# Values' products bound behind a feed-forward row, and the last weight splits put one in a slot

## The chip, the cores and the metric

The kernel runs on one core of one Trainium2 chip. The metric is the device time of one execution in microseconds. The kernel before takes 693.66 us, the median of three runs (693.4 to 695.26).

A core has five engines that run side by side, each through its own list of instructions in order: PE (TensorE, matrix products; its weight loads are shown apart as PEld), DVE (VectorE), ACT (ScalarE), POOL (GpSimd) and SP (SyncE, which issues the DMAs here). An engine that waits holds up all that stands behind in its list.

## The reference

Attention with four sink keys and a window of 128 keys, for 4 batches of 8 heads, 768 positions and 64 dimensions, and then a feed-forward layer on its output as 3072 tokens of 512 values:

```python
keep = is_sink | in_window                    # pos < 4, or 0 <= rel < 128
scores = np.where(keep, scale * q @ k.T, -1e9)
a = softmax(scores)
x = (a @ v).transpose(0, 2, 1, 3).reshape(3072, 512)
h = x @ w_in                                  # 512 x 2048
sp = np.maximum(h, 0.0) + np.log1p(np.exp(-np.abs(h)))
g = h * erf(sp)
return g @ w_out                              # 2048 x 512
```

## The kernel before

**Tiles and stages.** The tokens are worked in 12 groups of 256 (`g`; three groups make a batch). A group's attention takes four *steps*, one for each pair of heads, so that there are 48 steps `s`. Its feed-forward part takes 16 *rows* (`f`), one for each 128 of the 2048 hidden values; rows are counted through as `m = 16 * g + f`.

A step goes through all engines. PE makes the scores (`ps`, L420). DVE puts masks on them and takes the row's extreme (L433, L438), ACT the exponentials and their sum (L442, four a step), DVE divides by the sum (L454 to L476). From step 12 on DVE turns the result in blocks (`turn`, L489 and L490), and two DMAs through DRAM (`pd<-turn`, L492; `pa<-pd`, L518) finish the turn. POOL masks the two triangles of the window into `pz` and `pa` (L529, L533, L542). Then PE makes the values' products (`av`, L584), and ACT and DVE split them into a high and a low part (`xh`, L603; `xl`, L604), which are the input of the feed-forward rows of that group.

A row is 12 hidden products (`h`, L797: four parts of 128, three products of high and low each). Two rows share one buffer `h`, of which there are two, so a pair of rows needs the buffer of the pair but one before: ACT (L814) and DVE (L817) must have read that. ACT (L814 to L820) and DVE (L817, L821) make the activation of two rows; DVE casts its high part (L828) and POOL subtracts for the low part (L829, `g`). Four rows later come the projections (`o`, L844 to L846, six for a row), which sum up in two banks for each group; ACT copies them out (L850) before the next group uses the banks.

**The weights** are 32 blocks: 0 to 15 of `w_in`, 16 to 31 of `w_out`. Products of the first rows use them whole (`wf`); later ones use a high and a low part (`wt`), which `wsplit` makes once for each block: a cast on ACT (L708) and a subtract on DVE (L709). The table `split` says in which row that is due.

**The order.** Rows are written in slots `a = m + 10`. Each part of a slot is written under a priority (`at`), and a scheduler then sets every engine's order by priority and by when it thinks that the inputs are ready. `follow(prev, ins)` adds to that: `ins` comes after `prev`, with no wait on the chip where both are on one engine. `core(s)` writes the values' products of step `s - 2` and behind them the scores of step `s`; from step 8 on, step `s` has its slot at `a = 4 * s - 12`. In `av` the products are chained with `follow`; `prev` is what the first of them must come behind. `mark` keeps named instructions for that.

Of the kernel before, what the change touches and what calls it, by code (L numbers as in the profile page):

```python
# [39 lines left out]
NE, AL = 4, 2  # L40
# [3 lines left out]
DT = 10  # L44

TT, T2 = 12, 15

NSINK = 22

LATE = 31  # L50

FH = 8
# [10 lines left out]
def kernel(  # L63
# [11 lines left out]
    nc = tc.nc  # L75
# [3 lines left out]
    NPAIR = H // 2  # L79
    NC = DM // P  # L80
    NF = DF // P
# [59 lines left out]
    def fast_path():  # L141
        with ExitStack() as st:
# [64 lines left out]
            xp, early = {}, {}  # L207

            stp = {}
            mark = {}  # L210
            first, turn = [], []
# [127 lines left out]
            def warm(o, n):  # L339

                for _ in range(n):
                    nc.tensor.transpose(out=o, in_=ident, identity=ident)

            def follow(prev, ins):

                if prev is not None:
                    tc.add_manual_dep(
                        ins.ins, prev.ins.name,
                        mybir.DependencyInfo(mybir.DependencyClass.NoSync, mybir.DependencyReason.DATA), reason="order",
                    )  # L350
                return ins
# [23 lines left out]
            def core(s):  # L375

                prev = mark.get(("p", s - 1)) if s - AL == 3 * NPAIR - 1 else mark["av", s - 1] if s == 2 * NPAIR else None
                late = s - AL >= 2 * NPAIR and s - AL != 3 * NPAIR - 1
                if late:
                    prev = av(s - AL)  # L380
                if s < NSTEP:
                    score(s, prev)
# [63 lines left out]
            def turn_tile(tag):  # L446

                x = wpool.tile([P, 2 * DM], F32, name=f"turn_{len(turn)}", **tag)
                turn.append(x.rearrange("p (m t) -> p m t", t=P))
# [101 lines left out]
            def av(s):  # L551

                g, c = divmod(s, NPAIR)
                d = stp[s]
                gb = g % GPB
                if s < 2:
                    a = ps_h.tile([P, 2, GT], F32, tag="h", name=f"av_{s}")[:, 0, :]
                elif s < NE:
                    a = ps_o.tile([P, DM], F32, tag="o", name=f"av_{s}")[:, :GT]
                else:  # L560
                    a = ps_t.tile([P, GT], F32, tag="t", name=f"av_{s}")
                d["av"] = a
                vt, pz = d["v"], d["pz"]
                warm(a[:, :P], 6 if s < NE - 1 else 0)
                late = s >= TT and gb > 0
                pa = d["pa"].rearrange("p h i t -> p h (i t)")
                ops = []
                for j, (t0, t1) in enumerate(((0, HP), (HP, 3 * HP), (3 * HP, GT))):
                    if j > 0 or gb > 0:
                        x = vt[j] if isinstance(vt, list) else vt[:, j]  # L570
                        ops.append((x, pa[:, :, t0:t1], t0))
                if late:
                    ops = [ops[1], ops[0], ops[2]]
                for i in range(2):
                    for z, hf in enumerate((lo, hi)):
                        ops.append((vz[:, z, i, 2 * c : 2 * c + 2], pz[:, :, i, hf], P * i + HP * z))
                prev = mark.get(("p", s + 1)) if 0 < s < NE - 1 else None
                for m, (x, y, t0) in enumerate(ops):
                    for h in range(2):
                        o = a[64 * h : 64 * h + 64, t0 : t0 + y.shape[-1]]  # L580
                        with at(pos(s), "rest") if s >= TT and m + h > 0 else nullcontext():
                            prev = follow(
                                prev,
                                nc.tensor.matmul(  # L584
                                    o, x[:, h, :], y[:, h, :], start=(m == 0), stop=(m == len(ops) - 1), skip_group_check=True
                                ),
                            )
                mark["av", s] = prev
                return prev
# [16 lines left out]
            def at(a, what):  # L606

                key = int(a * PW) + O[what] + (E.get(what, 0) if a < EA else 0)
                return tc.high_priority(offset=tc.tile_snap_priority() + 1 - key)

            def pos(s):

                return s if s < NE else 3 * s - 6 if s < 2 * NPAIR else 4 * s - 12

            plan = {}
            for s in range(NSTEP + AL):
# [23 lines left out]
                if s < 2 * NPAIR:  # L640
                    x = pos(s) + (3 if s < NE else 5)
# [9 lines left out]
            def attn(a):  # L651

                for what, fn, s in sorted(plan.get(a, ()), key=lambda x: (STAGES.index(x[0]), x[2])):
                    with at(a, "prepl" if what == "prep" and s > TT else what):
                        fn(s)
# [3 lines left out]
            def need(n):  # L659
                return 4 * (n // 4) if n < 16 else n - 16 + LAG  # L660

            order = sorted(range(32), key=need)
            split = {}
            for n in range(32):
                x = n - 16
                split.setdefault(NF - 5 + n if x < 0 else NF + 6 + (x - FH) * 5 // 4 if x >= FH else 2 * NF - 1 + x * 2 // 3, []).append(n)

            def wload(n):

                src = wblock(n)  # L670
                t = staged[n] = wpool.tile([P, 2 * DM], I32, tag="wo", name=f"ws_{n}")
                if src.dtype == F32:
                    mark["wl"] = nc.sync.dma_start(t[:, :DM].bitcast(F32), src)
                else:
                    mark["wl"] = nc.sync.dma_start(t, src.bitcast(I32))
# [24 lines left out]
            def wsplit(n, m):  # L700

                t = wf[n]
                tag = dict(tag="wk", bufs=4) if n in (18, 20, 22) else dict(tag="wo")
                d = wt[n] = wpool.tile([P, 2, DM], F32R, name=f"wt_{n}", **tag)
                x, y = mlp.mark[min((m - 1) // 2, NF) - 1]
                if m >= LATE:
                    x, y = mark["e", 3 * NPAIR], mark["s", 3 * NPAIR]
                follow(x, nc.scalar.copy(d[:, 0, :], t))  # L708
                follow(y, nc.vector.tensor_tensor(d[:, 1, :], t, d[:, 0, :].bitcast(F32), op=ALU.subtract))  # L709

# [6 lines left out]
            mlp = make_mlp(work, ps_h, ps_o)  # L717
# [19 lines left out]
            for m in range(-LEAD, NG * NF + LAG + 2):  # L737
                a = m + LEAD
                live = 0 <= m < NG * NF
                if live:  # L740
                    g, f = divmod(m, NF)
                    if f % 2 == 0:
                        hp = mlp.hid_tile(m)
                    if f > 0:
                        with at(a, "hid"):
                            ahead = mlp.hidden(hp, xp[g], f)
                attn(a)
                if m == NF - 6:
                    turn_tile(dict(tag="wo"))
                w = m - LAG  # L750
                if 0 <= w < NG * NF:
                    g2, f2 = divmod(w, NF)
                    with at(a, "proj"):
                        mlp.project(gs[w // 2], g2, f2, lambda ins: follow(ahead if live and f and g >= 2 else None, ins))
                    if f2 == NF - 1:
                        for i in range(2):
                            r0 = (g2 * 2 + i) * P
                            with at(a, "res"):
                                nc.sync.dma_start(out[r0 : r0 + P, :], mlp.result(g2, i))
                if live:  # L760
                    if f == 0:
                        with at(a, "hid"):
                            mlp.hidden(hp, xp[g], f)
                    if f % 2 == 1:
                        with at(a, "act"):
                            gs[m // 2] = mlp.act(hp, m, m < NF + FH)

                while wn < 32 and a >= 1 and (wn < (0, 0, 3, 5)[a - 1] if a < 5 else wn < 2 * a - 4 or need(order[wn]) <= m + W1):
                    with at(a, "wc"):
                        wconv(order[wn], wn)  # L770
                    wn += 1
                    with at(a, "wl"):
                        for n in order[wl : wn + WQ]:
                            wload(n)
                            wl += 1
                for n in split.get(m, ()):
                    with at(a, "ws"):
                        wsplit(n, m)
# [74 lines left out]
    def general_path():  # L853

        NT_S = S // P
        with ExitStack() as st:
# [71 lines left out]
            with tc.tile_pool(name="g_one1", bufs=1) as one, tc.tile_pool(name="g_work1", bufs=2) as work:  # L928
# [3 lines left out]
                with tc.For_i(0, B, 1) as b:  # L932
                    for gb in range(GPB):
# [25 lines left out]
                        for i in range(2):  # L959
# [3 lines left out]
                            )  # L963

    fast_path()
    ok = nc.values_load(flagi[0:1, 0:1], min_val=0, max_val=1)
    with tc.If(ok == 0):
# [31 lines left out]
```

## Time and profile before

| | us |
|---|---|
| time, median of three runs | 693.66 |
| time of the profiled execution | 693.52 |
| its span on the core | 691.8 |
| PE busy in the span | 672.9 (97%) |
| ACT busy | 506.2 (73%) |
| DVE busy | 486.3 (70%) |
| POOL busy | 289.8 (42%) |

The span runs from the first to the last instruction of the profiled execution; 1.7 us of its time lie around it. Busy is time with an instruction of that engine at work. Matmuls overlap, and their ends are modelled, so two that follow each other are best measured from start to start. The granted clock of PE is 1.00 in nearly all of the span.

### The profile page before, as it was taken

The page shows a single profiled execution, that of the slowest core. Times are in us where ns is not written, and L with a number is a line of the kernel's source. Part 1 is how long each engine was busy: PE and PEld are TensorE (multiplying, and loading weights), DVE is VectorE, ACT ScalarE, POOL GpSimd, SP SyncE. Part 2 cuts the span into 40 slices and gives each one's busy share as a digit, 9 for nine tenths or more (in the row PEclk, how much of TensorE's full clock was granted, in tenths as well). Part 3 has the DMA queues.
Part 4 walks back from the last instruction along what each step waited for, and adds up shares of the span by engine and source line. Part 5 has one row for each costly group of instructions (what it writes and reads, how often), then busy time and mean ns, then how long its engine had stood idle before and what let it go on. Part 6 is the DMA issues. An engine that isn't in the chain of part 4 may idle for free.

```text
span 691.8 us, 16069 instructions
## 1 busy us (share of the span) xinstructions
PE 672.9 (97%) x5527; PEld 562.6 (81%) x5527; DVE 486.3 (70%) x1385; ACT 506.2 (73%) x1143; POOL 289.8 (42%) x510
## 2 busy tenths in 40 slices
PE   8899999999999999999999999999999999999996
PEld 5666567788787888898898898888898888899895
DVE  7999996769878788677685686577685678443241
ACT  5788668988876778687587587597596587587583
POOL 3422213133536545474464364355464364332231
PEclk9999999999999999999999999999999999999999
DMA  8999203114545655553553554353553464120001
GB/s 221 275 383 349 82 16 71 37 32 88 124 82 111 138 103 102 128 102 71 124 103 65 121 105 103 86 110 72 123 105 64 108 118 85 42 48 1 31 1 36
DMA packets 258873, 72.06 MB, mean 104 GB/s; under 512 B 224800, under 2 KB 250912, under 8 KB 258784
## 3 DMA queue, kind: packets, MB, share of 16 engines
q1 hardware_dynamic: 258224, 70.89, 44.0%
q8 instruction: 46, 0.75, 0.5%
q14 instruction: 43, 0.35, 0.2%
q10 hardware_dynamic: 560, 0.07, 0.1%
HBM read 51.25 MB, written 19.40 MB: 102 GB/s over the span
## 4 chain that ended last, share of the span: by engine, by line
PE 78%; DVE 8%; ACT 6%; DMA 4%; issue 2%; SPq 1%; POOL 1%; DVEq 0%; ACTq 0%; POOLq 0%
PE h L797 31%; PE o L844 10%; PE o L846 10%; PE o L845 10%; PE av L584 6%; PE ps L420 5%; PE o L841 3%; ACT pst L442 1%; DMA ws<-in_moe_w_out_dram 1%; DMA pa<-pd 1%; DMA pd<-turn 1%; PE h L793 1%; DVE wf L696 1%; DVE wf L693 1%; DVE pst L462 1%
## 5 line engine op out<-in xcount | busy, mean ns | idle before, releaser
L797 PE MATMUL h<-xh,wt 128*128 128x256 f32 x1408 | 271.8, 283 | 1.1 <-DVE w L817 1.1
L797 PEld LDWEIGHTS h<-xh,wt 128*128 128x128 f32 x1408 | 223.6, 188 | 17.8 <-issue 10.4
L797 PE MATMUL h<-xl,wt 128*128 128x256 f32 x704 | 196.5, 279 | 0.0
L829 POOL TENSOR_TENSOR g<-w,g 128x512 fp32r<-128x512 f32 x84 | 113.1, 1346 | 156.3 <-DVE g L828 155.2
L797 PEld LDWEIGHTS h<-xl,wt 128*128 128x128 f32 x704 | 132.5, 188 | 6.3 <-issue 2.4
L844 PE MATMUL o<-wt,g 128*128 128x512 f32 x336 | 131.9, 394 | 0.0
L845 PE MATMUL o<-wt,g 128*128 128x512 f32 x336 | 131.8, 392 | 0.0
L846 PE MATMUL o<-wt,g 128*128 128x512 f32 x336 | 129.0, 394 | 0.3 <-POOL g L829 0.3
L442 ACT ACTIVATE pst<-pst,neg 128x144 f32<-128x144 f32 x192 | 77.5, 405 | 55.9 <-DVE neg L438 55.6
L821 DVE SCALAR_TENSOR_TENSOR w<-u,w 128x512 f32<-128x512 f32 x84 | 73.9, 880 | 35.7 <-ACT u L820 35.6
L817 DVE SCALAR_TENSOR_TENSOR w<-w,h 128x512 f32<-128x512 f32 x84 | 56.7, 676 | 43.5 <-ACT w L816 41.0
L814 ACT ACTIVATE r<-h 128x512 f32<-128x512 f32 x96 | 57.0, 594 | 28.3 <-PE h L797 26.4
L828 DVE CAST g<-w 128x512 fp32r<-128x512 f32 x84 | 38.5, 458 | 52.8 <-PE o L846 49.6
L844 PEld LDWEIGHTS o<-wt,g 128*128 128x128 f32 x336 | 63.1, 188 | 12.5 <-issue 1.3
L846 PEld LDWEIGHTS o<-wt,g 128*128 128x128 f32 x336 | 62.3, 188 | 12.7 <-POOL g L829 0.7
L845 PEld LDWEIGHTS o<-wt,g 128*128 128x128 f32 x336 | 63.1, 188 | 9.6
L542 POOL TENSOR_SCALAR_AFFINE_SELECT pz<-pa 64x256 f32<-64x256 f32 (+1 forms) x96 | 43.8, 456 | 54.5 <-ACT pa L504 53.6
L820 ACT ACTIVATE u<-r 128x512 f32<-128x512 f32 x96 | 60.6, 632 | 6.1 <-DVE w L821 0.5
L816 ACT ACTIVATE w<-r 128x512 f32<-128x512 f32 x96 | 60.6, 631 | 3.2
L815 ACT ACTIVATE r<-r 128x512 f32<-128x512 f32 x96 | 60.6, 631 | 2.6
L819 ACT ACTIVATE r<-r 128x512 f32<-128x512 f32 x96 | 60.6, 632 | 2.4
L818 ACT ACTIVATE r<-r 128x512 f32<-128x512 f32 x96 | 60.5, 631 | 2.5
(107 smaller groups left out, 975.7 us busy)
## 6 DMA issues: line engine op xcount, KB each, us to landing
pd<-turn SPq DMA_DIRECT2D x36, 320.0 KB, 2.6
pa<-pd SPq DMA_DIRECT2D x144, 80.0 KB, 2.6
ws<-in_moe_w_in_dram SPq DMA_DIRECT2D x16, 512.0 KB, 6.6
ws<-in_moe_w_out_dram SPq DMA_DIRECT2D x16, 512.0 KB, 8.4
out_dram<-ot SPq DMA_DIRECT2D x24, 256.0 KB, 2.2
v<-in_v_dram SPq DMA_DIRECT2D x56, 96.0 KB, 2.6
kq<-in_k_dram SPq DMA_DIRECT2D x152, 32.0 KB, 1.9
kq<-in_q_dram SPq DMA_DIRECT2D x152, 32.0 KB, 2.2
```

The lines of the kernel that those rows point to most:

```text
L442: mark["e", s] = nc.scalar.activation(y, y, AF.Exp, bias=d["neg"][:, i, h : h + 1], scale=-1.0, accum_out=d["sum"][:, i, h : h + 1])
L797: last = nc.tensor.matmul(o, wt[NC * j + c][:, p, fs], xt[e][:, c, :], start=(m == 0), stop=(m == len(ops) - 1))
L815: nc.scalar.activation(r, r, AF.Square, bias=b_v, scale=-0.5)
L816: nc.scalar.activation(w, r, AF.Square, bias=b_w)
L818: nc.scalar.activation(r, r, AF.Square, bias=b_r)
L819: nc.scalar.activation(r, r, AF.Square, bias=b_q)
L820: sq = nc.scalar.activation(u, r, AF.Square, bias=b_u, scale=CK**0.5)
L821: pr = nc.vector.scalar_tensor_tensor(out=acc, in0=u, scalar=CU0 * CK, in1=acc, op0=ALU.add, op1=ALU.mult)
L829: nc.gpsimd.tensor_tensor(gl, acc, gh.bitcast(F32), op=ALU.subtract)
L844: behind(nc.tensor.matmul(o, gh[:, ws], wt[16 + f][:, 0, :], start=(f == 0), stop=False))
L845: nc.tensor.matmul(o, gh[:, ws], wt[16 + f][:, 1, :], start=False, stop=False)
L846: nc.tensor.matmul(o, gl[:, ws], wt[16 + f][:, 0, :], start=False, stop=(f == NF - 1))
```

## The change

It does four things. The values' products of steps 12 to 19 are put behind the last product of the hidden row that was written last before them (`mark["h"]`), in the same slot; they had no such bound. The blocks 16 to 23 become due in rows 30 to 37, one a row, where it was rows 31 to 35. Each split's cast and subtract follow the activation of the pair of rows before its own; a cap on that, and a rule that put all splits due from row 31 on behind the softmax of step 12, are gone. And the tile that step 12 turns into (`turn_0`) is allocated under the priority of the splits, with a memset of eight of its columns on POOL.

```diff
+BL = 20
@@ av
-                prev = mark.get(("p", s + 1)) if 0 < s < NE - 1 else None
+                prev = mark.get(("p", s + 1)) if 0 < s < NE - 1 else mark["h"] if TT <= s < BL else None
@@ the table split (NF = 16, FH = 8)
-                split.setdefault(NF - 5 + n if x < 0 else NF + 6 + (x - FH) * 5 // 4 if x >= FH else 2 * NF - 1 + x * 2 // 3, []).append(n)
+                split.setdefault(NF - 5 + n if x < 0 else NF + 6 + (x - FH) * 5 // 4 if x >= FH else 2 * NF - 2 + x, []).append(n)
@@ wsplit
-                x, y = mlp.mark[min((m - 1) // 2, NF) - 1]
-                if m >= LATE:
-                    x, y = mark["e", 3 * NPAIR], mark["s", 3 * NPAIR]
+                x, y = mlp.mark[(m - 1) // 2 - 1]
@@ the slots
-                            ahead = mlp.hidden(hp, xp[g], f)
+                            ahead = mark["h"] = mlp.hidden(hp, xp[g], f)
                 attn(a)
                 if m == NF - 6:
-                    turn_tile(dict(tag="wo"))
+                    with at(a, "ws"):
+                        turn_tile(dict(tag="wo"))
+                        nc.gpsimd.memset(turn[0][:, 5, :8], 0.0)
```

The scheduler orders the engines anew with this. The names in the rows below are the tiles': `av_12` belongs to step 12, `h_36` to rows 36 and 37, `wt_28` to block 28, `o_2_0` to group 2; the number at the end is the buffer's. Line numbers in the kernel after are two higher than before, but for L708 and L709, which are the same in both.

On ACT, around the softmax of step 12, before:

```order
L442 ACTIVATE pst_135,sum_12_1756<-pst_135,neg_12_1757 128x144
L603 CAST xh_2_1428<-av_11_1808 128x256
L442 ACTIVATE pst_135,sum_12_1756<-pst_135,neg_12_1757 128x144 x3
L708 CAST wt_28_1847<-wf_28_1028 128x512
L708 CAST wt_29_1878<-wf_28_1028 128x512
L708 CAST wt_30_1921<-wf_30_1044 128x512
L708 CAST wt_31_1969<-wf_30_1044 128x512
L708 CAST wt_16_2028<-wf_16_614 128x512
L708 CAST wt_17_2031<-wf_16_614 128x512
L814 ACTIVATE r_33_2089<-h_32_2034 128x512
```

And where four of these casts stand in the kernel after, around the softmax of step 11 and the activation of rows 28 and 29:

```order
L708 CAST wt_30_1922<-wf_30_1044 128x512
L708 CAST wt_16_1970<-wf_16_614 128x512
L444 ACTIVATE pst_135,sum_11_1569<-pst_135,neg_11_1570 128x144
L708 CAST wt_31_1973<-wf_30_1044 128x512
L444 ACTIVATE pst_135,sum_11_1569<-pst_135,neg_11_1570 128x144 x3
L816 ACTIVATE r_29_1908<-h_28_1851 128x512
L817 ACTIVATE r_29_1908<-r_29_1908 128x512
L818 ACTIVATE w_29_1909<-r_29_1908 128x512
L820 ACTIVATE r_29_1908<-r_29_1908 128x512
L821 ACTIVATE r_29_1908<-r_29_1908 128x512
L822 ACTIVATE u_29_1910<-r_29_1908 128x512
L708 CAST wt_17_2032<-wf_16_614 128x512
```

The block of six casts behind step 12 is taken apart; the casts stand ahead of step 12, among the work of steps 11 and 12.

On PE, at the values' products of step 12, before:

```order
L797 MATMUL h_36_2242<-xh_2_1428,wt_7_1413 128x256
L797 MATMUL h_36_2242<-xl_2_1429,wt_7_1413 128x256
L797 MATMUL h_36_2242<-xh_2_1428,wt_7_1413 128x256
L584 MATMUL av_12_2122<-pa_12_1865,v_12_1589 64x128 x2
L584 MATMUL av_12_2122<-pa_12_1865,v_12_1589 64x64 x2
L584 MATMUL av_12_2122<-pz_12_1991,vz_131 64x64 x8
L420 MATMUL ps_14_2137<-kq_130 64x144 x4
```

And in the kernel after, behind twelve projections of group 2's first two rows:

```order
L848 MATMUL o_2_1_2258<-wt_17_2032,g_33_2101 128x512
L799 MATMUL h_38_2311<-xh_2_1429,wt_4_1283 128x256
L799 MATMUL h_38_2311<-xl_2_1430,wt_4_1283 128x256
L799 MATMUL h_38_2311<-xh_2_1429,wt_4_1283 128x256
L799 MATMUL h_38_2311<-xh_2_1429,wt_5_1319 128x256
L799 MATMUL h_38_2311<-xl_2_1430,wt_5_1319 128x256
L799 MATMUL h_38_2311<-xh_2_1429,wt_5_1319 128x256
L586 MATMUL av_12_2120<-pa_12_1866,v_12_1590 64x128 x2
```

The products of step 12 move from the end of row 37 to the middle of row 38.

On PE, where group 2's projections end and group 3's begin, before:

```order
L845 MATMUL o_2_1_2263<-wt_31_1969,g_47_2777 128x512
L846 MATMUL o_2_1_2263<-wt_31_1969,g_47_2777 128x512
L584 MATMUL av_17_3048<-pa_17_2781,v_17_2537 64x128 x2
L584 MATMUL av_17_3048<-pa_17_2781,v_17_2537 64x64 x4
L584 MATMUL av_17_3048<-pz_17_2927,vz_131 64x64 x8
L420 MATMUL ps_19_3065<-kq_130 64x208 x2
L420 MATMUL ps_19_3065<-kq_130 64x224 x2
L420 MATMUL ps_19_3065<-kq_130 64x208 x2
L420 MATMUL ps_19_3065<-kq_130 64x224 x2
L844 MATMUL o_3_0_2987<-wt_16_2028,g_49_2843 128x512
```

And after:

```order
L848 MATMUL o_2_0_2257<-wt_31_1973,g_47_2778 128x512
L846 MATMUL o_2_1_2258<-wt_31_1973,g_47_2778 128x512
L847 MATMUL o_2_1_2258<-wt_31_1973,g_47_2778 128x512
L848 MATMUL o_2_1_2258<-wt_31_1973,g_47_2778 128x512
L846 MATMUL o_3_0_2988<-wt_16_1970,g_49_2844 128x512
L847 MATMUL o_3_0_2988<-wt_16_1970,g_49_2844 128x512
```

The products of step 17 and the scores of step 19 are no longer between the two groups' projections.

## Rows read from the trace of the kernel before

**Rows 1.** The page, part 1: busy us, share of the span, instructions.

```profile
PE 672.9 (97%) x5527; PEld 562.6 (81%) x5527; DVE 486.3 (70%) x1385; ACT 506.2 (73%) x1143; POOL 289.8 (42%) x510
```

**Rows 2.** Stretches: from:to, length, busy us (instructions), PE clock, DMA share, GB/s.

```profile
170.00:180.00 10.00, 8.48 (x91) 7.21 (x90) 9.70 (x28) 8.62 (x22) 5.89 (x13) 1.00 0.35 99
240.00:690.00 450.00, 446.19 (x3744) 390.59 (x3743) 285.28 (x807) 321.80 (x688) 205.49 (x344) 1.00 0.40 83
```

**Rows 3.** Timeline of PE: start, length, line, tiles, [idle before <-releaser].

```profile
173.76 0.34 PE L584 MATMUL av<-pa,v 128*64 128x64 f32 x4 [0.99 <-POOL pa L542]
...
177.02 0.36 PE L797 MATMUL h<-xh,wt 128*128 128x256 f32 x1 [0.53 <-DVE w L817]
...
206.36 0.39 PE L845 MATMUL o<-wt,g 128*128 128x512 f32 x1
206.59 0.40 PE L846 MATMUL o<-wt,g 128*128 128x512 f32 x1
207.59 0.39 PE L797 MATMUL h<-xh,wt 128*128 128x256 f32 x1 [0.61 <-DVE w L817]
...
211.46 0.72 PE L846 MATMUL o<-wt,g 128*128 128x512 f32 x2 [0.28 <-POOL g L829]
...
221.50 0.67 PE L584 MATMUL av<-pa,v 128*64 128x128 f32 x12 [1.03 <-POOL pa L542]
...
232.67 0.67 PE L584 MATMUL av<-pa,v 128*64 128x128 f32 x12 [0.96 <-POOL pa L542]
```

**Rows 4.** Timeline of ACT: casts of weights, exponentials of step 13.

```profile
159.36 3.21 ACT L708 CAST wt<-wf 128x512 fp32r<-128x512 f32 x6
...
170.58 0.41 ACT L442 ACTIVATE pst<-pst,neg 128x144 f32<-128x144 f32 x1
```

**Rows 5.** Stretches, columns PE, PEld, DVE, ACT, POOL as in rows 2.

```profile
137.00:155.00 18.00, 18.00 (x151) 14.16 (x151) 10.93 (x30) 16.67 (x35) 7.38 (x13) 1.00 0.16 31
```

**Rows 6.** Timelines of POOL and PE: step 11's last masks and products.

```profile
152.16 0.90 POOL L542 TENSOR_SCALAR_AFFINE_SELECT pa<-pa 64x256 f32<-64x256 f32 x2
...
156.27 0.67 PE L584 MATMUL av<-pa,v 128*64 128x64 f32 x12
```

**Rows 7.** Timelines of POOL and DVE at 210 us.

```profile
210.12 1.29 POOL L829 TENSOR_TENSOR g<-w,g 128x512 fp32r<-128x512 f32 x1
...
210.25 1.70 DVE L821 SCALAR_TENSOR_TENSOR w<-u,w 128x512 f32<-128x512 f32 x1
```

**Rows 8.** Line 709: ns min/median/max, first and last start.

```profile
L709 DVE TENSOR_TENSOR wt<-wf,wt x32: 643/685/897, 90.5 to 189.8; 128x512 fp32r<-128x512 f32 x32
```

**Rows 9.** The chain that ended last: start, us, what (paces of PE).

```profile
268.23 1.07 PE av L584 x28
269.30 0.92 PE ps L420 x16
...
412.34 1.38 PE h L797 x12
```

**Rows 10.** Timelines of PE and POOL: scores (12, 16), last masks (12, 22).

```profile
155.49 0.85 PE L420 MATMUL ps<-kq 64*64 64x144 f32 x16
...
173.40 0.31 POOL L542 TENSOR_SCALAR_AFFINE_SELECT pa<-pa 64x128 f32<-64x128 f32 x1
...
197.94 0.99 PE L420 MATMUL ps<-kq 64*64 64x208 f32 x16
...
285.29 0.90 POOL L542 TENSOR_SCALAR_AFFINE_SELECT pa<-pa 64x256 f32<-64x256 f32 x2
```

**Rows 11.** Timeline of ACT: exponentials of step 16, activation of row 44.

```profile
204.10 0.42 ACT L442 ACTIVATE pst<-pst,neg 128x144 f32<-128x144 f32 x1 [2.49 <-DVE neg L438]
...
204.92 0.61 ACT L816 ACTIVATE w<-r 128x512 f32<-128x512 f32 x1
```

**Rows 12.** Timeline of PE: a group's last projection and the next one's first.

```profile
649.71 0.40 PE L846 MATMUL o<-wt,g 128*128 128x512 f32 x1
650.14 0.50 PE L844 MATMUL o<-wt,g 128*128 128x512 f32 x1
```

## What the change was predicted to do

> **What bounds the kernel now.** I read the page's first part, then the busy time by stretch, then TensorE's waits one by one, then for each wait the rows of the engine that ended it. TensorE (PE) is busy 672.9 of 691.8 us [rows 1]. From 240 us on it is busy 446.2 of 450 us, and what is missing lies in the tail; between 170 and 180 us it is busy 8.5 of 10 [rows 2]. No PE work is added or taken out by the change, so it can win only where PE stands still, and the change moves instructions only between about 137 and 330 us. In that stretch PE has six waits, all before 240 us [rows 3]: three values' products (steps 12, 16 and 17) wait for a POOL mask of their `pa` tile, two hidden rows for VectorE's read of the hidden buffer they reuse (L817), one projection for POOL's low half (L829). The brackets add up to 0.99 + 0.53 + 0.61 + 0.28 + 1.03 + 0.96 = 4.40 us. A bracket counts from the modelled end of the matmul before, which is too late: projections follow each other every 0.23 us (206.36, 206.59), and the row after the one at 206.59 starts 1.00 us later, so 0.77 us are lost where the bracket says 0.61. With 0.16 us more for each, the six cost 5.4 us. That is the most the change can give back.
>
> **Part 1, the weights' last splits.** Nothing is added: the same 12 casts on ScalarE (L708) and subtracts on VectorE (L709), earlier. Now six casts stand in one row behind the softmax of step 12, 3.21 us, and six more between the activations that follow. The exponentials of step 13, whose scores PE does in that stretch, run only at 170.58 [rows 4]. In the new order eight of the twelve casts are ahead of the softmax of step 12. What this frees: ScalarE and VectorE between 160 and 177 us, hence the wait for L817 at 177.02 (0.70 us) and the late masks of steps 12 and 13. What it costs: ScalarE is busy 16.67 of 18 us between 137 and 155 us [rows 5], so six casts at 0.535 us each (3.21 us by six [rows 4]), 3.2 us, exceed the 1.3 us that are free there. First to feel it is step 11. Its masks end at 153.06 us, its products start at 156.27 [rows 6]: 3.2 us of cover. The new order takes 3.2 us of casts ahead of its copies on ScalarE and one 1.29 us POOL subtract (L829, the length at 210.12 [rows 7]) ahead of its last two masks, and gives 0.7 us because its products stand three projections later on PE. The balance is 3.2 - 3.2 - 1.3 + 0.7, a new wait of 0.6 us. Bounds: 0 (VectorE and ScalarE wait for PE at just this point) and 1.3 (the POOL subtract whole). I take 0.5.
>
> VectorE is busy 10.93 of the 18 us there [rows 5], and eight subtracts at 0.69 us [rows 8] add 5.5 to 7.1 free, so I put them at nothing; they are hidden by VectorE's own idle time, and without it they would reach the L817 that releases each hidden buffer. One row speaks against that: at 210.25 an L821 on VectorE took 1.70 us beside a POOL L829 of 1.29 us that had begun just before it; it ended 0.5 us after it [rows 7]. The Trainium skill (page "SBUF — State Buffer", section "SBUF: two separate sides") says that GpSimd and a VectorE instruction with two SBUF inputs hold a shared port pair in turn, each for its whole length. The row agrees. By that rule the moved subtracts, which have two SBUF inputs, would each be held up to 1.29 us where a POOL subtract runs, three times in this stretch, and VectorE would be 2 us short instead of 1.6 us free. That is the second rival below.
>
> The new memset of eight columns of the turn tile goes to POOL ahead of the masks of step 7; I found nothing late that it waits for. I put it at nothing, since POOL is busy 42% of the span [rows 1]; without that cover it costs what the smallest POOL rows here take, 0.3 us (173.40 [rows 10]).
>
> **Part 2, the values' products.** The binding is a bound from below. The order shows what it does after the scheduler has filled in the rest: the products of step 12 come behind two projection pairs and half a hidden row, those of step 17 behind two pairs and row 54. The products of 13 and 15 come earlier than before. What counts is the PE work between a step's scores and its products, since the round trip through softmax, transposes, two DMAs and POOL must fit in there. I count it in the two orders at the trace's paces [rows 9]: 0.115 us for a hidden product (1.38 by 12), 0.23 for a projection, 1.07 and 0.92 for a step's products and scores. Steps 12 to 23, before: 16.7, 24.7, 21.2, 20.6, 20.4, 15.6, 18.9, 20.3, 23.8, 25.4, 18.0, 23.6 us. After: 19.4, 18.7, 20.8, 18.8, 18.2, 24.7, 24.8, 24.9, 19.4, 20.4, 16.7, 19.9. The round trip itself, from the first score product to the end of the last mask, was 18.2 us in step 12, 23.5 in step 16 (its products, at 221.50 [rows 3], waited for that mask) and 17.0 in step 22 (scores in [rows 9], masks in [rows 10]).
>
> Step 12: 19.4 against 18.2, even with the late exponentials of part 1; its 1.2 us go. Step 17 has 24.7; its 1.1 go. Step 16 gets less room, 18.2. Its trip was long because VectorE stood with its L821 for 1.70 us, two POOL subtracts of 1.3 us each came in between, and ScalarE waited 2.49 us for step 16's row maxima [rows 7, 11]. In the new order ScalarE does the four remaining activations of row 44 before these exponentials, which frees the buffer for row 48 (the 0.77 us at 207.59) and, with it, the projection at 211.46 (0.4). I estimate a trip of 18.5 and take a wait of 0.3 here; the bounds are 0 (17.0, step 22's) and 5.3 (23.5, its own).
>
> Two new costs. Group 3's first projection now follows directly on group 2's last, where the products and scores of steps 17 and 19 stood between. It reuses the bank that L850 has to copy out first. The same pattern stands at 649.71 and 650.14: 0.43 us instead of 0.23 [rows 12]; 0.2 us, bounds 0 and 0.4 (the copy begins later). And step 22 has 16.7 us for a trip of 17.0, and its exponentials stand behind five more activations of 0.61 us (the length at 204.92 [rows 11]) on ScalarE. Bounds 0.3 and 0.3 + 3.1; since those activations are early too, I take 0.8.
>
> **Sum.** -5.4 + 0.5 + 0.3 + 0.2 + 0.8 = -3.6 us. The profiled execution took 693.52 us (span 691.8 and 1.7 around it), the median is 693.66: 693.5 - 3.6 = 689.9 us.
>
> **The rivals.** *The stall moves, no measurable change.* The casts and subtracts meet a busy ScalarE and POOL's port (by the skill's rule above), so that VectorE falls 2 us behind and releases a hidden buffer late: PE waits some 2 us at rows 32 to 34, and the trips of 16 and 22 stay 1.5 us too long. New waits 2 + 1.5 + 1.5 + 0.2 = 5.2, less 5.4: 693.3 us; half of it gives 691.9. For: ScalarE's full stretch, the L821 at 210.25. Against: VectorE has 7 us free, and PE's buffers are released 2 us ahead there. The case that the change doesn't do what it says leads to the same place: if the three waits for masks (3.5 us by the rows) only follow their products, and splits alone help, it is 5.4 - 3.5 - 0.7, some 692.3.
>
> *The round trip keeps its length, slower.* Steps 15 and 16 both get tighter (20.6 to 18.8, 20.4 to 18.2). If both took the 23.5 us that step 16 took, PE would wait 4.7 + 5.3 = 10.0 us, and with the other costs of 1.5 the time is 693.5 - 5.4 + 10.0 + 1.5 = 699.6. It decides against the change from 7.5 us of such waits, that is from trips over 22.2 us. For: the trace has such a trip. Against: its causes are queue positions that the new order changes, and step 12 and 22 did it in 17 to 18 us.
>
> **How the numbers follow.** A measurement of this kernel tells about 0.3% (2.1 us) from no change. Forecast, 688.1 to 691.5 us: 0.60, all of it faster. The moved stall, 691.6 to 693.8: 0.30, the same. The kept round trip, above 695.7: 0.10. The range 688.0 to 693.9 takes in the first two: its low end is all six waits gone and nothing new, its high end the moved stall whole.
>
> **What would show it.** Right: PE idle between 170 and 240 us at 1 to 2 us instead of 4.4; no wait for L542 at the products of 12 and 17; no block of six L708; exponentials of step 13 within 5 us of their scores; PE as full after 240 us as now, but for a short wait at step 22. Wrong: a wait for L542 at steps 15, 16 or 22 of over 1 us, or PE waits for L817 or L603 between 145 and 165 us. Scores that wait on ScalarE would show as a long idle ahead of L442.

## The result: 0.7% slower, and the profile after

The changed kernel took 698.59 us (median; 697.83 to 700.09) beside 693.78 us for the kernel before on the same chip: a ratio of 1.007, 95% interval 1.0056 to 1.0084. The forecast was 689.9. The profiled execution took 698.36 us, with a span of 696.7 us, 4.9 more than before.

The page, part 1, of the changed kernel (busy us, share, instructions) answers to [rows 1]:

```profile
PE 675.2 (97%) x5527; PEld 564.3 (81%) x5527; DVE 485.2 (70%) x1385; ACT 505.5 (73%) x1143; POOL 295.9 (42%) x511
```

The number of matmuls is the same, but PE was busy 2.3 us longer: some of them were slower. The windows of the changed kernel say where (stretch, length, busy us of PE, PEld, DVE, ACT and POOL with instructions, granted clock, DMA share, GB/s):

```profile
170.00:180.00 10.00, 8.19 (x76) 6.46 (x78) 6.40 (x16) 7.84 (x15) 7.30 (x13) 1.00 0.63 148
200.00:240.00 40.00, 38.98 (x366) 33.35 (x365) 28.00 (x81) 25.05 (x59) 20.20 (x38) 1.00 0.60 123
286.00:293.00 7.00, 3.70 (x52) 2.66 (x44) 5.42 (x20) 3.94 (x13) 3.29 (x8) 1.00 0.71 169
293.00:297.00 4.00, 4.00 (x30) 2.55 (x24) 1.93 (x4) 3.61 (x7) 0.45 (x2) 0.57 0.34 72
297.00:690.00 393.00, 392.96 (x3257) 345.08 (x3254) 245.22 (x691) 281.74 (x599) 179.09 (x299) 1.00 0.39 80
```

From 170 to 180 us PE is no fuller than before (8.19 against 8.48 us [rows 2]). From 286 to 293 it stands still for 3.3 of 7 us, and in the four microseconds after that the granted clock is 0.57 on average. Before, PE was full from 240 us on, but for the tail [rows 2]. From 297 us on it is as full as before: the loss is made by then.

PE's waits one by one (timeline of PE, changed kernel; L586 are the values' products, L544 the POOL masks, L831 POOL's low half, L846 to L848 the projection, L422 the scores, those at 262.75 and 271.52 of steps 21 and 22):

```profile
172.83 0.50 PE L846 MATMUL o<-wt,g 128*128 128x512 f32 x1 [0.17 <-ACT ot L852]
173.17 0.40 PE L847 MATMUL o<-wt,g 128*128 128x512 f32 x1
175.20 0.73 PE L848 MATMUL o<-wt,g 128*128 128x512 f32 x2 [1.63 <-POOL g L831]
...
208.60 0.65 PE L586 MATMUL av<-pa,v 128*64 128x128 f32 x6 [0.98 <-POOL pa L544]
...
230.40 0.40 PE L848 MATMUL o<-wt,g 128*128 128x512 f32 x1
230.83 0.50 PE L846 MATMUL o<-wt,g 128*128 128x512 f32 x1
...
262.75 0.99 PE L422 MATMUL ps<-kq 64*64 64x208 f32 x16
...
270.45 0.67 PE L586 MATMUL av<-pa,v 128*64 128x128 f32 x12 [0.89 <-POOL pa L544]
...
271.52 0.99 PE L422 MATMUL ps<-kq 64*64 64x208 f32 x16
...
288.35 0.40 PE L848 MATMUL o<-wt,g 128*128 128x512 f32 x1
292.05 0.67 PE L586 MATMUL av<-pa,v 128*64 128x128 f32 x12 [3.30 <-POOL pa L544]
...
293.11 0.69 PE L846 MATMUL o<-wt,g 128*128 128x512 f32 x1
293.60 0.63 PE L847 MATMUL o<-wt,g 128*128 128x512 f32 x1
294.03 0.63 PE L848 MATMUL o<-wt,g 128*128 128x512 f32 x1
...
295.87 1.22 PE L422 MATMUL ps<-kq 64*64 64x144 f32 x16
297.01 0.39 PE L799 MATMUL h<-xh,wt 128*128 128x256 f32 x1
```

All six waits of [rows 3] are gone. Six others are there, with 0.16 us more than each bracket as before: 0.34 and 1.80 (172 to 175 us, a projection), 1.15 (step 15's products), 0.21 (group 3's first projection), 1.04 (step 20), 3.46 (step 22). Right behind the last one projections follow each other every 0.43 us where 0.23 is the rule. With the scores behind them that costs 1.5 us: from step 22's products to the next hidden product it is 4.96 us here (292.05 to 297.01), and the same instructions take 3.44 us at the full clock in a kernel shown below (binding alone). The expectations of the experiments put this cost at 2.24 us, some 0.7 too much. New: 9.5 us. Gone: 5.4. The difference, 4.1, is most of the 4.9 us between the spans; the other 0.8 lies in many small amounts.

Why step 22 is late shows on VectorE and in its neighbour's loads. Timeline of VectorE, changed kernel, and behind it POOL's subtract beside L464 and its last masks of step 22:

```profile
277.25 0.71 DVE L361 STREAM_TRANSPOSE kq<-kq 128x512 f32<-128x512 f32 x1 [1.70 <-DMA kq<-in_q_dram]
...
279.19 2.79 DVE L464 TENSOR_SCALAR pst<-pst,sum 128x128 f32<-128x128 f32 x4
...
282.33 0.70 DVE L491 STREAM_TRANSPOSE turn<-pst 128x512 f32<-128x512 f32 x1
```

```profile
280.08 1.28 POOL L831 TENSOR_TENSOR g<-w,g 128x512 fp32r<-128x512 f32 x1
...
291.02 0.97 POOL L544 TENSOR_SCALAR_AFFINE_SELECT pa<-pa 64x256 f32<-64x256 f32 x2
```

Timeline of SyncE's DMA queue, changed kernel, and then the same two instructions in the kernel before:

```profile
272.14 1.49 SPq L494 DMA_DIRECT2D pd<-turn  x1
273.68 2.12 SPq L241 DMA_DIRECT2D kq<-in_q_dram  x4
```

```profile
264.44 0.38 SPq L492 DMA_DIRECT2D pd<-turn  x1
264.87 2.15 SPq L239 DMA_DIRECT2D kq<-in_q_dram  x4
```

The scores of steps 21 and 22 in the kernel before, timeline of PE:

```profile
255.58 0.99 PE L420 MATMUL ps<-kq 64*64 64x208 f32 x16
...
269.23 0.99 PE L420 MATMUL ps<-kq 64*64 64x208 f32 x16
```

The transposes of step 23's k and q (L361) stand on VectorE ahead of step 22's normalization (L464). They wait for step 23's q, whose loads the kernel binds behind the store of step 21's turned tile (`pd`). Before, that store was issued 4.8 us ahead of step 22's first score (264.44 and 269.23); now 0.6 us behind it (272.14 and 271.52). The scores of steps 21 and 22 lie 8.8 us apart instead of 13.7. So step 22's exponentials end at 277.19 us, but VectorE begins to turn its tile only at 282.33; its trip takes 20.5 us (271.52 to 291.99, the end of its last masks) instead of 17.0.

Of the 5.1 us from the exponentials to the turning, 1.70 are VectorE's idle time ahead of L361, and 1.9 are lost in the four L464, which took 2.79 us where 0.88 is usual. The second of them alone took 2.05 us and ended at 281.45, just behind three POOL instructions in a row, the last of them the L831 that ended at 281.36. The Trainium skill (page "SBUF — State Buffer", section "SBUF: two separate sides") says that GpSimd and a VectorE instruction that runs in a 2-port performance mode, or has two SBUF inputs, hold a shared port pair in turn, each for its whole length. The row fits this if L464 runs in such a mode, which no trace here shows.

### The profile page after: what moved, and what is told of

Same layout as the page of the kernel before. It is cut to its first block, busy times and chain, and to the rows that moved or that the text cites. A ratio compares the mean times of both kernels' runs of the same rounds, so it can differ in the third digit from the quotient of the medians.

```text
span 696.7 us, 16068 instructions
## 1 busy us (share of the span) xinstructions
PE 675.2 (97%) x5527; PEld 564.3 (81%) x5527; DVE 485.2 (70%) x1385; ACT 505.5 (73%) x1143; POOL 295.9 (42%) x511
## 4 chain that ended last, share of the span: by engine, by line
PE 72%; DVE 10%; ACT 9%; DMA 3%; issue 2%; POOL 1%; SPq 1%; DVEq 0%; POOLq 0%; ACTq 0%
PE h L799 29%; PE o L848 10%; PE o L846 10%; PE o L847 10%; PE av L586 5%; PE ps L422 5%; DVE wf L695 2%; DVE wf L698 2%; PE o L843 2%; DVE wf L690 1%; ACT wt L708 1%; DMA pd<-turn 1%; DMA pa<-pd 1%; ACT w L818 1%; ACT pst L444 1%
## 5 line engine op out<-in xcount | busy, mean ns | idle before, releaser
L831 POOL TENSOR_TENSOR g<-w,g 128x512 fp32r<-128x512 f32 x84 | 114.1, 1358 | 158.4 <-DVE g L830 157.0
L846 PE MATMUL o<-wt,g 128*128 128x512 f32 x336 | 133.3, 397 | 0.3 <-ACT ot L852 0.2
L848 PE MATMUL o<-wt,g 128*128 128x512 f32 x336 | 130.2, 395 | 1.6 <-POOL g L831 1.6
L823 DVE SCALAR_TENSOR_TENSOR w<-u,w 128x512 f32<-128x512 f32 x84 | 70.5, 839 | 38.9 <-ACT u L822 38.5
L848 PEld LDWEIGHTS o<-wt,g 128*128 128x128 f32 x336 | 62.9, 189 | 14.5 <-POOL g L831 2.1
L846 PEld LDWEIGHTS o<-wt,g 128*128 128x128 f32 x336 | 63.2, 188 | 13.1 <-ACT ot L852 1.6
L544 POOL TENSOR_SCALAR_AFFINE_SELECT pz<-pa 64x256 f32<-64x256 f32 (+1 forms) x96 | 48.8, 508 | 55.2 <-ACT pa L506 54.3
L535 POOL COPY pz<-pa 64x256 f32<-64x256 f32 x72 | 33.3, 463 | 74.1 <-DMA pa<-pd 72.1
L820 ACT ACTIVATE r<-r 128x512 f32<-128x512 f32 x96 | 60.6, 631 | 2.7
L817 ACT ACTIVATE r<-r 128x512 f32<-128x512 f32 x96 | 60.6, 632 | 2.5
```

What stands on the lines that cost most here:

```text
L817: nc.scalar.activation(r, r, AF.Square, bias=b_v, scale=-0.5)
L820: nc.scalar.activation(r, r, AF.Square, bias=b_r)
L823: pr = nc.vector.scalar_tensor_tensor(out=acc, in0=u, scalar=CU0 * CK, in1=acc, op0=ALU.add, op1=ALU.mult)
L831: nc.gpsimd.tensor_tensor(gl, acc, gh.bitcast(F32), op=ALU.subtract)
L846: behind(nc.tensor.matmul(o, gh[:, ws], wt[16 + f][:, 0, :], start=(f == 0), stop=False))
L848: nc.tensor.matmul(o, gl[:, ws], wt[16 + f][:, 0, :], start=False, stop=(f == NF - 1))
```

## The experiments

Ratios are to the kernel before, run on the same chip beside each kernel. They weigh all runs of both, and so differ a little from the quotient of the two medians. The median of the kernel before was 694.4 us for the first four kernels, 694.5 for the next four, 693.9 and 694.1 for the others.

**Which part costs.** Two kernels, the splits alone (with the turn tile's new place) and the binding alone. The first:

```diff
-  prev = mark.get(("p", s + 1)) if 0 < s < NE - 1 else mark["h"] if TT <= s < BL else None
+  prev = mark.get(("p", s + 1)) if 0 < s < NE - 1 else None
```

> The change without the binding: the earlier splits and the turn tile's new place alone. Theory A (the end of the binding squeezes step 22): step 22 has 19.4 us of PE work between scores and products instead of 16.7, so neither its wait of 3.46 us nor the low clock of 2.24 us behind it comes; the wait of 1.80 us at 175 us stays, and step 18, with 15.2 us, takes some 2 us. Sum against the kernel before: -5.4 + 2.1 (172 to 175 us) + 2.3 (steps 16 and 17 wait as before) + 2 = +1.0, some 694 to 695 us. Theory B (the earlier casts and subtracts cost the time): it is as slow as the changed kernel, 697 us or more.

Measured 694.65 us, ratio 0.9994 (0.9974 to 1.0014). Its waits lay elsewhere than I said (step 15 2.26 us, step 18 1.11, 1.54 at 172 to 175 us, none at steps 16 and 17), and step 22 had none. The profiled execution, with 695.55 us above the median, had a stretch at half the clock behind step 15's wait, which I hadn't expected either (timeline of PE, then its window):

```profile
209.63 0.71 PE L586 MATMUL av<-pa,v 128*64 128x128 f32 x8 [2.10 <-POOL pa L544]
```

```profile
209.60:213.60 4.00, 3.97 (x44) 2.85 (x45) 1.37 (x4) 1.53 (x3) 2.63 (x5) 0.59 0.59 131
```

The second kernel is the one before, with `mark["h"]` and the binding's line added, and nothing else:

> The binding alone, splits and turn tile as in the kernel before. Theory A: step 22 has 16.7 us again and waits 3 us or more with half the clock behind it, 5 us in all; the waits of steps 16 and 17 go (2.3 us), so 693.8 - 2.3 + 5.5 = 697 us, and the 1.80 us at 175 us do not come. Theory B: 691 to 693.8 us, no wait over 1 us at step 22.

Measured 700.66 us, ratio 1.0070 (1.0047 to 1.0093). By the times, the splits by themselves cost nothing that the runs can tell, and the binding by itself costs as much as the whole change. By the traces, two of the changed kernel's waits still belong to the splits: those at 172 to 175 us and step 15's are there with the splits alone, and not with the binding alone, where the waits of 173.76 and 177.02 stayed. Timeline of PE, binding alone:

```profile
289.57 0.40 PE L848 MATMUL o<-wt,g 128*128 128x512 f32 x1
292.70 0.67 PE L586 MATMUL av<-pa,v 128*64 128x128 f32 x12 [2.72 <-POOL pa L544]
...
296.14 0.38 PE L799 MATMUL h<-xh,wt 128*128 128x256 f32 x1
```

Theory A has its wait. The clock stayed at 1.00 behind it in this execution, which took 697.29 us; nine of the twelve runs took 699.9 to 701.8. What these nine had more isn't seen, since only one execution of a kernel has a trace.

**Where the binding ends.** Three kernels with another `BL`, and the binding alone without an end:

```diff
-BL = 20
+BL = 48
```

> The change with the binding carried on to the last step, so that it has no end at step 20: PE work between scores and products is 24.8 to 24.9 us for every step from 17 on. Theory A: the waits of steps 20 and 22 (1.04 and 3.46 us) and the low clock (2.24 us) go, 698.6 - 6.7 = 691.9 us; the 1.80 us at 175 us and the 1.15 us of step 15 stay. Theory B, or a round trip that is long for another cause: 697 us or more, with a wait for POOL's masks at some later step.

Measured 695.21 us, ratio 1.0011 (0.9992 to 1.0030), 3.4 us less than the changed kernel's 698.59. Windows of this kernel:

```profile
175.00:179.00 4.00, 4.00 (x13) 3.30 (x14) 1.84 (x4) 3.03 (x5) 2.43 (x5) 0.57 0.74 203
285.00:293.00 8.00, 8.00 (x86) 6.98 (x85) 3.35 (x6) 5.95 (x11) 2.00 (x3) 1.00 0.74 174
```

PE is full where step 22 stood, and there is no wait above 0.3 us from 180 us to the end. So step 22 is late because the binding ends at step 20. The time still isn't 691.9. The expectation gave back some 0.7 us too much for the clock, and the trace shows three things more: half the clock now follows the wait at 175 us; PE's work itself, waits and low clock left out, takes some 4 us longer in many small amounts; and from the last projection's end to the end of the span it is 6.6 us instead of 5.6. Of the 4 us, 1.2 are in eight groups whose first projection stands right behind the last one of the group before, mostly 0.38 us instead of 0.23. The rest I could not put down to anything.

> The binding alone, carried on to the last step, with the splits as in the kernel before. Theory A: the waits of steps 16 and 17 go (2.3 us), those at 173.76 and 177.02 us (1.9 us) stay, and nothing new comes: 691 to 692.5 us, clock 1.00 from 240 us on. Theory B says the same within 1 us; if it is 695 us or more, the binding itself costs time and not its end.

Measured 696.81 us, ratio 1.0028 (1.0011 to 1.0045): the forecast was wrong. Step 16's products waited 2.16 us (1.19 before), the granted clock was 0.62 in the 4.5 us behind, and PE's work, waits and low clock left out, is again slower, by 3 to 4 us. Timeline of PE:

```profile
222.74 0.99 PE L586 MATMUL av<-pa,v 128*64 128x128 f32 x12 [2.00 <-POOL pa L544]
```

The binding alone is no gain here even without an end, and why PE's work is slower with it stays open.

```diff
-BL = 20
+BL = 24
```

> The change with the binding ended at step 24 instead of 20. Work between scores and products is 24.9 us for steps 20 to 23, and 19.2, 20.4, 18.1, 19.5 us for steps 24 to 27. Theory A (the end of the binding squeezes the steps behind it): no wait at steps 20 and 22 and no low clock there, a new wait of up to 1.5 us at step 26 with 18.1 us, 698.6 - 6.7 + 1 = 693 us. Rival (what is slow is the place in the program, at step 22, and not the end of the binding): the wait at 285 to 295 us stays, 697 us or more.

Measured 696.69 us, ratio 1.0030 (1.0002 to 1.0057). Nothing waits at steps 20 and 22. The wait went where theory A put it, to the step with 18.1 us behind the new end (timeline of PE, step 26):

```profile
326.49 0.77 PE L586 MATMUL av<-pa,v 128*64 128x128 f32 x8 [1.07 <-POOL pa L544]
...
328.16 0.85 PE L422 MATMUL ps<-kq 64*64 64x144 f32 x16 [0.44 <-POOL kq L375]
```

The time is 3.7 us above what I expected. Of that, 0.7 is the clock's price in the expectation, and part is half the clock behind the wait that ends at 177.5 us (window of this kernel); the rest stays open, with six runs from 694.1 to 698.3.

```profile
177.50:181.00 3.50, 3.48 (x9) 2.76 (x10) 1.42 (x3) 2.72 (x5) 2.08 (x5) 0.53 0.69 172
```

```diff
-BL = 20
+BL = 18
```

> The change with the binding ended at step 18: steps 16 and 17 keep the places of the changed kernel (18.2 and 24.7 us of work between scores and products), steps 18 to 22 get 17.9, 19.4, 23.6, 22.2, 18.0. Theory A: step 22 has what it had before the change, and no wait; step 18 waits 1 to 2 us, the 1.80 us at 175 us and the 1.15 us of step 15 stay: 693.8 - 5.4 + 2.1 + 1.15 + 1.5 = 693 us. Rival: a binding at any step costs the time that the changed kernel lost, 697 us or more.

Measured 694.29 us, ratio 0.9997 (0.9978 to 1.0017). Step 22 doesn't wait; step 18 waits 0.91 us, step 15 now 2.64, and the clock stays at 1.00 behind it:

```profile
210.46 0.71 PE L586 MATMUL av<-pa,v 128*64 128x128 f32 x8 [2.48 <-POOL pa L544]
```

**The clock.** Transposes ahead of step 22's products:

```diff
-  warm(a[:, :P], 6 if s < NE - 1 else 0)
+  warm(a[:, :P], 28 if s == 22 else 6 if s < NE - 1 else 0)
```

> The changed kernel with 28 more transposes of the identity (0.109 us each, 3.05 us) on TensorE ahead of step 22's products, into the bank that these write anyway; the result is the same. They fill the wait of 3.46 us and change no instruction ahead of it. Theory C (TensorE standing still for 3.3 us is what halves the granted clock): the wait is filled, the masks of step 22 come no earlier, but the clock stays at 1.00 behind it, 698.6 - 2.2 = 696.4 us. Rival (the low clock comes with or without that idle time, as at 24 us in the kernel before): a stretch at 0.5 is in the trace near 293 us all the same, 698.6 us.

Measured 696.39 us, ratio 1.0043 (1.0025 to 1.0060). Windows of this kernel:

```profile
173.00:180.00 7.00, 5.36 (x21) 3.87 (x21) 3.41 (x7) 5.26 (x9) 4.64 (x8) 0.76 0.71 176
285.00:293.00 8.00, 8.00 (x80) 6.47 (x79) 4.56 (x18) 5.00 (x15) 2.87 (x5) 1.00 0.66 145
293.00:297.00 4.00, 4.00 (x36) 3.91 (x35) 3.48 (x9) 3.81 (x7) 3.71 (x9) 1.00 0.56 146
```

With PE busy the clock stayed at 1.00. That the time is the expected one is luck: the 2.2 us taken off were too many, and this execution has half the clock at 175 us, which the changed kernel had not. And the edit did more than I said: the scheduler also put projections and hidden products between the transposes, and step 22's products came at 297.34, 2.3 us behind their masks. The run fits theory C and doesn't prove it, since with the binding alone the clock stayed at 1.00 behind a standstill of 2.72 us too.

**What VectorE waits for.** Step 23's loads of q bound behind an earlier store (the kernel e4_q of the later expectations):

```diff
-  last = mark.get(("d", s - 2))
+  last = mark.get(("d", s - 2 if s != 23 else s - 3))
```

> The changed kernel with the loads of step 23's q no longer bound behind the store of step 21's turned tile, but behind step 20's. Theory D (VectorE's 1.70 us of idle ahead of the transposes of step 23's k and q, which stand ahead of step 22's normalization, is what makes step 22 late): these transposes start as soon as they are reached, the wait at step 22 falls from 3.46 to 1.8 us or less, and with it the low clock may go: 694.7 to 697 us. Rival (the 16.7 us of work between scores and products are too few in any case, whatever VectorE waits for): the wait stays at 3 us or more and the time at 698 us or more.

Measured 696.00 us, ratio 1.0034 (1.0009 to 1.0060). Timelines of VectorE, then of PE:

```profile
276.62 0.71 DVE L361 STREAM_TRANSPOSE kq<-kq 128x512 f32<-128x512 f32 x1
...
278.89 0.88 DVE L464 TENSOR_SCALAR pst<-pst,sum 128x128 f32<-128x128 f32 x4
...
279.88 0.70 DVE L491 STREAM_TRANSPOSE turn<-pst 128x512 f32<-128x512 f32 x1
```

```profile
290.81 0.67 PE L586 MATMUL av<-pa,v 128*64 128x128 f32 x12 [0.63 <-POOL pa L544]
```

VectorE waits no longer, the turning of step 22 begins 1.5 us behind its exponentials instead of 5.1, and PE's wait is 0.79 us instead of 3.46, with about as much PE work between scores and products (17.4 us here, 17.1 in the changed kernel). Theory D stands: the room was short, but what made it cost 3.46 us was a load bound to the step before. The edit took away the idle time and the slow L464 together (0.88 us again), so that it doesn't tell the two apart. The time is still above the kernel before; in the profiled execution half the clock follows the wait at 175 us (0.62 on average from 175.5 to 180 us).

**The wait at 175 us.** I first took it for the same thing, a step's loads bound too late, and was wrong. The kernel q14_23, against e4_q:

```diff
-  last = mark.get(("d", s - 2 if s != 23 else s - 3))
+  last = mark.get(("d", s - 2 if s not in (14, 23) else s - 3))
```

> The kernel of e4_q with step 14's q loads unbound from the store of step 12's turned tile as well. Theory D again: VectorE's 1.93 us of idle ahead of step 14's transposes at 168.7 us goes, POOL runs step 13's and 12's work earlier and the low half of g (L831) ahead of step 12's masks, so the wait of 1.3 to 1.8 us at 175 us falls to 0.5 us or less, and no stretch at half the clock follows it: 696.0 - 1.3 - 1.7 = 693.0 us. Rival (POOL's queue of masks is what is late there, with or without the loads): the wait stays at 1 us or more and the time at 695.5 us or more.

Measured 694.80 us, ratio 1.0016 (1.0001 to 1.0030), but the wait had not gone. Timelines of POOL, then of PE:

```profile
172.06 0.72 POOL L531 COPY pz<-pa 64x128 f32<-64x128 f32 x1 [1.71 <-DMA pa<-pd]
...
173.37 1.26 POOL L831 TENSOR_TENSOR g<-w,g 128x512 fp32r<-128x512 f32 x1
```

```profile
174.69 0.50 PE L848 MATMUL o<-wt,g 128*128 128x512 f32 x1 [1.93 <-POOL g L831]
```

POOL's low half of row 33 (its input was ready at 170.6) stands behind step 12's copies, which wait for a DMA. So the last kernel keeps the one unbound load of step 23 and puts the low half ahead of them; the other copies and the masks of step 12 get the same `follow`, and they are written three slots later:

```diff
-  nc.gpsimd.tensor_copy(pz[hf, :, :, other], y.broadcast_to([HP, 2, 2, HP]))
+  follow(mlp.low if s == TT else None, nc.gpsimd.tensor_copy(pz[hf, :, :, other], y.broadcast_to([HP, 2, 2, HP])))
...
-  plan.setdefault(pos(s) + 5, []).append(("phalf", phalf, s))
+  plan.setdefault(pos(s) + (8 if s == TT else 5), []).append(("phalf", phalf, s))
-  nc.gpsimd.tensor_tensor(gl, acc, gh.bitcast(F32), op=ALU.subtract)
+  self.low = nc.gpsimd.tensor_tensor(gl, acc, gh.bitcast(F32), op=ALU.subtract)
```

> The kernel of e4_q, and on POOL the low half of row 33's g (L831) stands ahead of step 12's copies and masks instead of between them; no other engine's order changes at that place. Theory E (the 1.80 us at 175 us are the old wait for step 12's masks, moved to a projection whose low half is queued behind these masks): the projection's wait falls to 0.5 us or less, and step 12's products, 20.3 us behind their scores, wait 0 to 1.3 us for masks that now end 1.3 us later. Without the low clock that followed: 696.0 - 1.3 - 1.7 + 0.6 = 693.6 us. Rival (the low half itself comes late from VectorE, whatever is queued on POOL): the wait at 175 us stays over 1 us and the time at 695.5 us or more.

Measured 694.40 us, ratio 1.0003 (0.9990 to 1.0016). Timelines of POOL, then of PE:

```profile
171.97 1.30 POOL L832 TENSOR_TENSOR g<-w,g 128x512 fp32r<-128x512 f32 x1 [0.36 <-DVE sum L456]
```

```profile
176.65 0.36 PE L800 MATMUL h<-xh,wt 128*128 128x256 f32 x1 [0.76 <-DVE w L820]
```

The projection waits no more, nor do step 12's products at 178.4 us; the clock stays at 1.00. Theory E stands. In its place PE waits 0.92 us for VectorE's read of a hidden buffer, the very wait that stood at 177.02 before [rows 3]. Steps 15, 20 and 22 still wait (brackets of 1.42, 0.61 and 0.72 us). With both causes taken away the change is level with the kernel before, and no faster.

**A faster version.** Two kernels join the unbound load of step 14 to the splits alone, and to the end at 18 (bl18):

> The earlier splits without any binding of products, and step 14's q loads unbound as in q14_23. The waits at 172 to 175 us (1.5 us in the kernel without the binding) go to 0.5 us; step 15's wait of 2.26 us and step 18's of 1.11 us stay or change by a microsecond with the new positions: 694.65 - 1.0 = 693.6 us, not told from the kernel before. Below 692.5 us step 15's wait has gone too.

Measured 693.59 us, ratio 0.9991 (0.9980 to 1.0002).

> The change with the binding ended at step 18, and step 14's q loads unbound. From bl18: the waits at 172 to 175 us (1.5 us) go to 0.5 us, step 15's 2.64 us and step 18's 1.4 us stay: 694.3 - 1.0 = 693.3 us. If step 15 is not late, as in e4_q, 691 us, which would be faster than the kernel before.

Measured 693.61 us, ratio 0.9992 (0.9981 to 1.0004). Both take back the loss, and neither can be told from the kernel before. The times are the expected ones and the reason isn't: the wait at 175 us, which was to fall to 0.5 us, is 2.33 and 2.15 us, and what fell instead are the waits of step 15 (2.26 us to none, and 2.64 to 2.10) and of step 18 (1.11 us to 0.51, and 0.91 to none). Timelines of PE, first and second kernel:

```profile
175.21 0.79 PE L848 MATMUL o<-wt,g 128*128 128x512 f32 x1 [2.17 <-POOL g L831]
```

```profile
175.11 0.50 PE L848 MATMUL o<-wt,g 128*128 128x512 f32 x1 [1.99 <-POOL g L831]
```

## Why the prediction was wrong

- **Step 22, the term that failed.** I put it at 0.8 us: 16.7 us of room against a trip of 17.0, measured in the order before. It cost 3.46, and 1.5 more for the clock. The room was about right (17.1 measured); the trip was not a constant, and took 20.5. I had counted the PE work from each step's scores to its own products, and not the distance from one step's scores to the next one's. That distance decides when the neighbour's loads can start, and they stand ahead of the step on VectorE. The list of rooms could have warned: at the end of the binding step 19's products, and with them step 21's scores, are pushed back, and step 20's products with step 22's scores are not, so that steps 21 and 22 are squeezed together. The upper bound I gave, 3.4, is nearly the wait, and the sum took the lower part of the bounds. The prediction's own sign of being wrong, a wait of over 1 us at step 15 or 22, came at both.
- **The clock had no term.** A standstill of 3.3 us was in my bounds, and what it does to the matmuls behind it, 1.5 us, was not.
- **The six waits, 5.4 us: right as far as they go.** Three products, two hidden rows and a projection no longer wait where they did. But those of 173.76 and 177.02 (1.9 us) came back as 0.34 and 1.80. The prediction moved the products behind work that should cover the masks, and did not ask what this work waits for: a projection whose low half is queued on POOL behind the same masks. The rival "the stall moves" had a stall move, but on another engine: it named VectorE and the hidden buffers, and POOL's order was the one.
- **Steps 15 and 20, no term, 1.15 and 1.04 us.** I measured three trips and took them for all. Step 15's own trip before was 21.5 us (from its scores at 190.95 to the end of its masks at 212.49), and I left it 18.8. What made step 20's trip long isn't followed up.
- **Small terms.** Step 11: 0.5 forecast, 0 measured (masks end at 156.35, products start at 156.38). Step 16: 0.3, and 0. Group 3's first projection: 0.2, and 0.21.
- **The whole gap.** Forecast -3.6, measured +4.9 by the spans. Step 22 makes 2.7 of these 8.5 us, the clock 1.5, the two waits that came back 2.1, steps 15 and 20 together 2.2, and the small terms give back 0.8. Some 0.8 us stay open.
- **Two sums among the rivals.** Half of the moved stall gives 690.7 us, not 691.9. And the kept round trip is told from no change at some 6.1 us of waits, trips of 21.6 us, since the 7.5 leave out the 1.5 us of other costs. Neither changes the forecast.
- **The rival that came nearest**, the kept round trip, with a chance of 0.10, had the right kind of cause, a trip too long for its room, at steps 15 and 16. Step 22's trip was not kept, though: it grew by 3.5 us.

## What to carry to other kernels

Work between a producer and its consumer hides a trip only if it lasts as long as the trip. Before using a measured trip in a new order, follow each engine's queue on it, and ask which loads of the neighbouring steps stand in it and what releases them. Where a rule is applied to a range of steps, look first at the steps behind its end: here these got the smallest distances. And ask of the work that is to cover a wait whether it depends on the same queue.

## What was not expected of the hardware

A short standstill of PE can cost more than itself, and not each time. In the fourteen traces, from 130 us on, PE waits 17 times with a bracket of 1.15 us or more. Right behind eight of these waits the granted clock falls to half for some microseconds, and it falls nowhere else in that part of the traces before the tail. The length of the wait doesn't decide: it fell behind waits of 1.16, 1.20, 1.64, 1.65, 2.00, 2.10, 2.17 and 3.30 us, and not behind 1.15, 1.42, 1.63, 1.76, 1.93, 1.94, 1.99, 2.48 and 2.72 us. At one place, before the projection at 175 us, 1.63 us in the changed kernel left it at 1.00, and 1.64 us in the kernel with the transposes brought six projections at 0.43 us.

The price was 1.5 us behind step 22, six projections and the scores, against the same instructions at the full clock with the binding alone. So a wait of this length can be worth more in a sum than its own microseconds. Runs of one kernel spread by more than that (692.5 to 698.4 us for the kernel before); whether the clock makes this spread isn't shown, since one execution of each kernel has a trace.
